# All column-tiled leftovers of an FFN in one place, four live transposed chunks, and edits in the first ten microseconds

## Chip, core and metric

The kernel runs on one core of one Trainium2 chip. The metric is device microseconds of one execution. "PE" is TensorE's matmul row in a profile, "PEld" its weight loads, "DVE" VectorE, "ACT" ScalarE, "POOL" GpSimd, "SPq" the queue that issues transfers. PSUM is the memory that TensorE writes its products to. "Before" and "after" are the two profiled kernels.

## What is computed

A layer norm of x (2048 x 512), then the sum of x, a diagonal state-space branch and a SwiGLU feed-forward branch on the normed x:

```python
xn = _layernorm(x, axis=-1)
# branch A: h[t] = Lam_bar * h[t-1] + (xn @ B_bar^T)[t]; complex, 512 states
y  = 2.0 * einsum("blp,dp->bld", hseq, Cmat).real + xn * Dskip
# branch B: F = 1376
f  = (silu(xn @ w_gate) * (xn @ w_up)) @ w_down
return x + y + f
```

1376 is ten tiles of 128 and a leftover of 96. The kernel computes in bf16 with float32 accumulation, in four chunks of 512 positions, each of four tiles of 128. Below, xn is the normed x and xnT its transpose, "the scan" the recurrence h, and "the down product" the one with w_down.

## The kernel before

A small list scheduler orders every engine's instructions; TensorE and the transfer queue keep program order. Three parts matter.

Leftovers. The 96 leftover gate columns are filled up to 128 with 32 of the leftover up columns. The other 64 up columns are **column-tiled**: two chunks are multiplied at once, one into PSUM partitions 0 to 63, one into 64 to 127. It is done once for chunks 0 and 1, once for 2 and 3:

```python
def ffn_left(c):
    bk = next_pair()
    for k in range(2):                     # L839: full width, 4 matmuls per chunk
        ... e.matmul(pbank[:, bk + k, :], lhsT=wg[:, kt, FL*128:FT*128], rhs=xnT[:, (c + k) % 2, :, kt, :], ...)
    bu = next_pair()
    def mmu(e):                            # L849: 64 columns, two chunks side by side
        for kt in range(KT):
            for k in range(2):
                inst = e.matmul(pbank[64*k:64*k + NU0, bu, :], lhsT=wu[:, kt, FL*128:FL*128 + NU0],
                                rhs=xnT[:, (c + k) % 2, :, kt, :], ...)
    ...                                    # ACT evacuates, DVE multiplies into hT[:, :, FL, :]
```

Program order (cut):

```python
ffn_gate_quarters([0, 1, 2, 3])            # the head: chunk 0's first gate products, tile by tile
...
u1 = ssm_b_chunk(1)
ffn_left(0)
xt_chunk_dma(2)                            # transposed chunk 2 takes the buffer of chunk 0
...
dc_chunk(0)
...
ln_chunk(3); xt_chunk_dma(3)
...
dc_chunk(1)
...
ffn_left(2)
```

Head. Chunk 0's four tiles are normed and transposed on TensorE, between 128-column gate matmuls. Tile 0 is normed half by VectorE, half by ScalarE. Each pair of transposes needs the PSUM slot that ScalarE empties of the pair before. Until there is data, TensorE runs filler matmuls to bring its clock up.

```python
xt_tile_fine(0, 0, wbank)
pe_warm(1, 256, tiles[-2][1])
xt_tile_fine(0, 1)
pe_warm(1, 256, tiles[-2][1])
# (tile quarter, k, position among the gate tiles) -> (x tile, half) to be transposed there
place = {(0, 2, 4): (1, 0), (1, 0, 2): (1, 1), (1, 2, 2): (2, 0), (2, 0, 2): (2, 1), (2, 2, 1): (3, 0), (3, 0, 1): (3, 1)}
```

## Time and profile before

| | before |
|---|---|
| time, median of 3 runs | 179.07 us (179.02 to 179.21) |
| span of the profiled run | 177.7 us |
| PE / DVE / ACT busy | 98% / 92% / 49% |
| first, last matmul | 0.83, 175.11 us |
| clock of TensorE full from | 6.23 us |

The page says that PE bounds the kernel. Whether PE's time is dense, the prediction reads from the trace.

### The profile page before, as it was taken

To read this page: it belongs to the slowest core of one execution; us is meant where nothing else is said; L and a number is where in the kernel's file an instruction comes from. 1 tells how busy PE (TensorE), PEld (TensorE's weight loads), DVE (VectorE), ACT (ScalarE), POOL (GpSimd) and SP (SyncE) were. 2 spreads that over 40 slices of the span, in tenths; PEclk is the share of its full clock that TensorE was granted. 3 is DMA by queue.
4 is the path that set the end of the run, shared out by engine and by line. 5 is a ranking of instruction groups with operands and counts; after the bars stand their busy time and mean duration, and the time that the engine had idled before them with its cause. 6 is when DMAs were issued, how large, how long until landed. Compare 5 with 4: busy or idle time off the path is not lost.

```text
span 177.7 us, 2429 instructions
## 1 busy us (share of the span) xinstructions
PE 174.5 (98%) x935; PEld 84.3 (47%) x935; DVE 162.7 (92%) x284; ACT 87.6 (49%) x116; POOL 10.2 (6%) x22
## 2 busy tenths in 40 slices
PE   8999999999999999999999999999999999999994
PEld 2894444444444444444444444444444444444743
DVE  2865999999999999999999999999999999999933
ACT  4679979899999591052565560000965520000000
POOL 3040500040000000400000000000000000000000
DMA  5892795664956000002600000002000000001122
GB/s 161 268 371 80 132 133 112 163 131 102 348 127 48 0 0 0 0 30 92 120 0 0 0 0 4 0 24 93 1 0 4 0 0 0 0 0 35 36 81 89
DMA packets 22966, 12.37 MB, mean 70 GB/s; under 512 B 15180, under 2 KB 22956, under 8 KB 22956
## 3 DMA queue, kind: packets, MB, share of 16 engines
q1 hardware_dynamic: 22652, 11.77, 26.4%
q10 hardware_dynamic: 304, 0.46, 0.8%
q8 instruction: 7, 0.11, 0.3%
q14 instruction: 3, 0.02, 0.0%
HBM read 6.46 MB, written 2.10 MB: 48 GB/s over the span
## 4 chain that ended last, share of the span: by engine, by line
PE 98%; DVE 0%; issue 0%
PE pb L759 36%; PE pb L959 21%; PE pb L972 16%; PE pb L876 16%; PE pb L803 4%; PE pb L477 3%; PE pb L839 2%; PE pb L849 1%; PE pb L582 1%; DVE x_sb L977 0%
## 5 line engine op out<-in xcount | busy, mean ns | idle before, releaser
L916 DVE TENSOR_TENSOR_SCAN rot<-sm,car,rot 128x512 bf16<-128x512 f32 x32 | 38.8, 1265 | 0.1
L959 PE MATMUL pb<-wd,hT 128*128 128x512 bf16 (+3 forms) x198 | 38.8, 355 | 0.0
L759 PE MATMUL pb<-xnT,wu 128*128 128x512 bf16 x160 | 37.3, 379 | 0.0
L759 PE MATMUL pb<-xnT,wg 128*128 128x512 bf16 x132 | 31.3, 379 | 0.0
L972 PE MATMUL pb<-W,hss 128*128 128x512 bf16 (+2 forms) x144 | 28.3, 355 | 0.0
L876 PE MATMUL pb<-xnT,BT 128*128 128x512 bf16 x128 | 28.1, 379 | 0.0
L959 PEld LDWEIGHTS pb<-wd,hT 128*128 128x128 bf16 (+1 forms) x198 | 18.5, 98 | 19.9
L771 ACT ACTIVATE sg<-pb 128x1024 bf16<-128x1024 f32 x20 | 20.1, 1023 | 9.6 <-PE pb L759 8.7
L759 PEld LDWEIGHTS pb<-xnT,wu 128*128 128x128 bf16 x160 | 15.7, 98 | 18.9 <-issue 0.2
L829 ACT ACTIVATE uf<-pb 128x1024 bf16<-128x1024 f32 x20 | 20.5, 1024 | 7.8 <-PE pb L759 6.8
L972 PEld LDWEIGHTS pb<-W,hss 128*128 128x128 bf16 x144 | 13.5, 98 | 14.3
L759 PEld LDWEIGHTS pb<-xnT,wg 128*128 128x128 bf16 x132 | 12.7, 98 | 15.7 <-issue 0.8
L876 PEld LDWEIGHTS pb<-xnT,BT 128*128 128x128 bf16 x128 | 12.5, 98 | 15.1
L883 ACT ACTIVATE u_sb<-pb 128x1024 bf16<-128x1024 f32 x16 | 16.2, 1016 | 4.4 <-PE pb L876 4.4
L977 DVE TENSOR_TENSOR x_sb<-pb,x_sb 128x512 bf16<-128x512 f32 (+2 forms) x18 | 11.1, 624 | 4.3 <-PE pb L972 4.1
L831 DVE TENSOR_TENSOR hT<-sg,uf 128x1024 bf16<-128x1024 bf16 x20 | 13.5, 681 | 0.8 <-ACT uf L829 0.6
L506 ACT ACTIVATE xn_sb<-x_sb,nmr,rstd 128x512 bf16<-128x512 bf16 x8 | 5.9, 802 | 10.2 <-DVE nmr L503 10.2
L858 ACT ACTIVATE sg<-pb 96x1024 bf16<-96x1024 f32 x2 | 2.0, 1020 | 17.1 <-PE pb L839 17.1
L907 DVE TENSOR_TENSOR rot<-rot,cosT 128x2048 bf16<-128x2048 bf16 x8 | 9.7, 1214 | 0.1
L907 DVE TENSOR_TENSOR rot<-rot,sin 128x2048 bf16<-128x2048 bf16 x8 | 9.7, 1218 | 0.0
L907 DVE TENSOR_TENSOR rot<-u_sb,cosT 128x2048 bf16<-128x2048 bf16 x8 | 9.7, 1216 | 0.0
L907 DVE TENSOR_TENSOR rot<-u_sb,sin 128x2048 bf16<-128x2048 bf16 x8 | 9.7, 1216 | 0.0
(81 smaller groups left out, 143.3 us busy)
## 6 DMA issues: line engine op xcount, KB each, us to landing
out_dram<-x_sb SPq DMA_DIRECT2D x15, 128.0 KB, 1.7
x_sb<-in_A_x_dram SPq DMA_DIRECT2D x3, 512.0 KB, 7.1
wd<-in_B_w_down_dram SPq DMA_DIRECT2D x1, 1280.0 KB, 6.4
wu<-in_B_w_up_dram SPq DMA_DIRECT2D x1, 768.0 KB, 5.3
wu<-in_B_w_up_dram SPq DMA_DIRECT2D x1, 608.0 KB, 7.4
x_sb<-in_A_x_dram SPq DMA_DIRECT2D x4, 128.0 KB, 3.3
wg<-in_B_w_gate_dram SPq DMA_DIRECT2D x1, 480.0 KB, 6.3
wg<-in_B_w_gate_dram ACTq DMA_DIRECT2D x1, 448.0 KB, 3.9
```

The source lines that it names most:

```text
L759: inst = e.matmul(pbank[0:fs, bk, :].rearrange("p (j t) -> p j t", j=4), lhsT=w[:, kt, i * 128:i * 128 + fs], rhs=xnT[:, c % 2, :, kt, :], ...
L771: g.add("act", lambda e: e.activation(out=sg[rows, sl, 0:n, :].rearrange("p a t -> p (a t)"), in_=pair_f32(rows, bk, 512 * n), func=AF.Sil ...
L803: inst = e.matmul(pbank[:, bk, q * 128:(q + 1) * 128], lhsT=wg[:, kt, i * 128:(i + 1) * 128], rhs=xnT[:, 0, q, kt, :], start=(kt == 0), st ...
L829: g.add("act", lambda e: e.activation(out=uf[rows, ul, 0:n, :].rearrange("p a t -> p (a t)"), in_=pair_f32(rows, bk, 512 * n), func=AF.Ide ...
L831: g.add("dve", lambda e: e.tensor_tensor(out=hT[rows, hb, i0:i0 + n, :], in0=sg[rows, sl, 0:n, :], in1=uf[rows, ul, 0:n, :], op=ALU.mult), ...
L876: inst = e.matmul(pbank[:, bk, :].rearrange("p (j t) -> p j t", j=4), lhsT=BT[:, ri, kt, pt * 128:(pt + 1) * 128], rhs=xnT[:, c % 2, :, kt ...
L883: g.add("act", lambda e: e.activation(out=u_sb[:, us].rearrange("p r t -> p (r t)"), in_=pair_f32(slice(0, 128), b0), func=AF.Identity), r ...
L907: tt = lambda out, a, b, op, r, w, nm: g.add("dve", lambda e: e.tensor_tensor(out=out, in0=a, in1=b, op=op), reads=r, writes=w, name="%s_% ...
L916: g.add("dve", lambda e, A0=A0, A1=A1, k=k, ri=ri, pt=pt: e.tensor_tensor_scan(out=A1[:, k, ri, :], data0=rr[:, pt:pt + 1].to_broadcast([1 ...
L959: inst = e.matmul(pbank[:, bk, 0:nc_], lhsT=hT[0:fs, hb, i, lt * 128:(lt + 1) * 128], rhs=wd[0:fs, i, c0:c0 + nc_], start=(i == 0), stop=F ...
L972: inst = e.matmul(pbank[:, bk, 0:nc_], lhsT=hss[:, hb, pt, ri, lt * 128:(lt + 1) * 128], rhs=W12[:, ri, pt, c0:c0 + nc_], start=False, sto ...
L977: g.add("dve", lambda e, bk=bk, a=a, c0=c0, nc_=nc_: e.tensor_tensor(out=x_sb[:, a, c0:c0 + nc_], in0=pbank[:, bk, 0:nc_], in1=x_sb[:, a, ...
```

## The change

Its intent: do the column-tiled matmuls of all four chunks in one run. That needs chunks 0 to 3 transposed and alive at the same time (so four xnT: that of chunk 2 lies in table scratch, that of chunk 3 in a buffer that first holds the iota), chunk 3's x, norm and transpose much sooner, and the down weights later. Two edits of the head come along, and with that of tile 0 a third, small one: tile 1's statistics in one instruction.

```diff
-        xnT = sb("xnT", [128, 2, 4, KT, 128], B16)
+        xnT01 = sb("xnT", [128, 2, 4, KT, 128], B16)
+        xnT3 = sb("xnT3", [128, 4, KT, 128], B16)
+        xnT2 = scrC[:, 2048:3072].bitcast(B16)...          # aliases table scratch; xnT3 also serves as iota
+        xnT = [xnT01[:, 0], xnT01[:, 1], xnT2, xnT3]
...
@@ loads_stage_b2
             dma("ld_x8", ...)
+            dma("ld_x12", ...)
+            dma("ld_dsk", ...)
             dma("ld_cre", ...); dma("ld_cim", ...)
-            dma("ld_wd0", ...); dma("ld_wd1", ...); dma("ld_x12", ...); dma("ld_dsk", ...)
...
@@ head
-            cs = slice(h * 256, (h + 1) * 256)
+            cs = slice(0, 384) if a == 0 else slice(h * 256, (h + 1) * 256)
...                                                          # ScalarE: columns 384:512 instead of 256:512;
...                                                          # tile 1's statistics in one instruction, not two
-            place = {..., (1, 2, 2): (2, 0), ...}
+            place = {..., (1, 2, 1): (2, 0), ...}
...
@@ ffn_left
-        def ffn_left(c):
+        def ffn_left():                                      # all gate leftovers, then all column-tiled ones
+            for c in (0, 2): ... 8 full-width matmuls
+            for c in (0, 2): ... 8 column-tiled matmuls
...                                                          # result in hL; the down product of it now comes
...                                                          # just before the scan outputs (mmB), not last of mmA
@@ program order
         u1 = ssm_b_chunk(1)
-        ffn_left(0)
         xt_chunk_dma(2)
+        dma("ld_wd0", ...); dma("ld_wd1", ...)
...
         resid_chunk(0)
+        ln_chunk(3)
+        xt_chunk_dma(3)
+        ffn_left()
         dc_chunk(0)
...
         resid_chunk(1)
-        ln_chunk(3)
-        xt_chunk_dma(3)
...
-        ffn_left(2)
```

The number of matmuls stays 935.

## The prediction

> **What bounds the kernel now.** I read first the page of the profile: shares of busy time and the chain that ended last.
>
> ```profile
> span 177.7 us, 2429 instructions
> PE 174.5 (98%) x935; PEld 84.3 (47%) x935; DVE 162.7 (92%) x284; ACT 87.6 (49%) x116; POOL 10.2 (6%) x22
> PE 98%; DVE 0%; issue 0%
> ```
>
> The chain is PE from 0.83 us to 175.34 us. "Busy" alone proves little, since the ends of matmuls are modelled, so I listed the start-to-start distance of every matmul in the trace. Warm, a 128x512 matmul follows its predecessor after 0.216 us and a 128x128 one after 0.056 us. Past the head, and apart from the narrower matmuls of the end, that holds everywhere except around the two blocks of column-tiled leftovers. So PE never waits for DVE, ACT or a DMA after 13 us: only fewer PE slots, cheaper PE slots or an earlier head can shorten this kernel. I looked for these in the timeline.
>
> The two leftover blocks (L839 full-width gate part, L849 column-tiled up part, then the next L759), from the timeline:
>
> ```profile
> 38.13 1.89 PE L839 MATMUL pb<-xnT,wg 128*128 128x512 bf16 x8
> 39.95 1.05 PE L849 MATMUL pb<-xnT,wu 128*64 128x512 bf16 x8
> 40.93 1.90 PE L759 MATMUL pb<-xnT,wg 128*128 128x512 bf16 x8
> ...
> 122.13 1.89 PE L839 MATMUL pb<-xnT,wg 128*128 128x512 bf16 x8
> ...
> 123.95 1.05 PE L849 MATMUL pb<-xnT,wu 128*64 128x512 bf16 x8
> ...
> 124.94 0.61 PE L759 MATMUL pb<-xnT,wg 128*128 128x512 bf16 x2
> ```
>
> Subtract the starts. The eight full-width ones take 39.95-38.13 = 1.82 us, where 8 x 0.216 = 1.73 would do: 0.09 too much. The eight half-width ones run as four pairs (the two of a pair start 3 ns apart) and take 0.98 us, where 4 x 0.216 = 0.86 would do: 0.12 too much. Each block so costs about 0.21 us beyond its work, and the second repeats the first.
>
> The head, tiles 0 and 2 of the first chunk, from the timeline:
>
> ```profile
> 4.42 0.35 DVE L517 TENSOR_SCALAR xn_sb<-x_sb,mv,rstd 128x256 bf16<-128x256 bf16 x1
> ...
> 4.74 0.60 ACT L548 ACTIVATE xn_sb<-x_sb,nm,rstd 128x256 bf16<-128x256 bf16 x1
> ...
> 4.84 0.42 PE L582 MATMUL pb<-ident,xn_sb 128*128 128x128 bf16 x2
> ...
> 5.39 0.13 PEld L582 LDWEIGHTS pb<-ident,xn_sb 128*128 128x128 bf16 x2 [0.30 <-ACT xn_sb L548]
> ...
> 8.95 0.83 PE L803 MATMUL pb<-xnT,wg 128*128 128x128 bf16 x12
> 9.15 0.45 ACT L592 ACTIVATE xnT<-pb 128x128 bf16<-128x128 bf16 x2 [0.62 <-PE pb L582]
> ...
> 9.74 0.27 PE L582 MATMUL pb<-ident,xn_sb 128*128 128x128 bf16 x2
> ```
>
> Tile 0's second half waits for ScalarE: it ends at 4.74+0.60 = 5.34 us and PE starts at 5.40. Tile 2's second transposes start at 9.74, but the twelve matmuls before them take only 12 x 0.056 = 0.67 from 8.95, to 9.62. The 0.12 us between is a wait for the PSUM slot that ScalarE empties at 9.15+0.45 = 9.60.
>
> **What the Trainium skill says.** "TensorEngine Tiling (Array Packing)", Key Properties: a change of tiling mode drains TensorE. This trace agrees: 0.310 us instead of 0.216 at entry into the column-tiled run, 0.237 for its first pair, 0.313 at exit, and no extra between later pairs. "TensorE: Matmul & The Clock Gate", the section on 56 ns: warm spacing 55.6 and 215.7 ns, cold 106.7 ns; the trace agrees, with 107 ns for 128 columns until 6.23 us and 56 after. The same page, "What's actually happening": the cold phase is a budget of time (about 3.4 us), not a number of matmuls. The trace shows 5.4 us of cold from the first matmul, longer; I keep only that it is time. "VectorE: DVE Perf Modes", the errata section: instructions on SBUF pay a fixed cost on top of their width. The trace agrees: VectorE's normalisation repeats after 0.262 us at 256 columns and 0.324 at 512, ScalarE takes 0.599 and 0.805.
>
> **The change, part by part.**
>
> 1. Leftovers in one place. Removed from PE: nothing in number (16+16 leftover matmuls stay; the down-projection's leftover matmul moves from before the scan outputs to their group). But 16 column-tiled matmuls now run in a row, so one entry and one exit go: (0.310-0.216)+(0.237-0.216)+(0.313-0.216) = 0.21 us, all on the path, since PE is the path.
>
> 2. Tile 0, 384 to VectorE and 128 to ScalarE. VectorE: +128 columns at (0.324-0.262)/256 a column = +0.03 us, so the first transposes go from 4.84 to 4.87. ScalarE: -128 columns at (0.805-0.599)/256 = -0.10, so its part ends at 5.24. PE can then do the first two transposes and a warm filler, 4.87+0.21+0.21 = 5.30, and goes on at once instead of at 5.40. Two cold transposes and one filler later (2 x 0.107+0.213) the first real matmul starts at 5.73 instead of 5.80. These 0.07 us are cold: if the clock rises at a fixed time, the work pulled ahead is worth half, 0.04 us. Tile 1's statistics in one instruction (0.73 to the next, against 0.78 for two) pay back VectorE's 0.03.
>
> 3. Tile 2's transposes one gate tile (two matmuls, 0.11 us) sooner: ScalarE empties the slot that much sooner and the 0.12 us wait goes. Its input is ready (VectorE ends at 8.53, the new place is about 8.7 us). Tile 3's next transposes wait for a ScalarE square root that is queued behind the same evacuation, so they move too. Worth 0.12, about.
>
> 4. Chunk 3's normalisation, xnT3, x12 and dsk earlier, wd later, aliases instead of own buffers: no PE work. Worth 0 if nothing comes late.
>
> Sum: 0.21+0.04+0.12 = 0.37 us. From 179.07: **178.7 us**.
>
> **Does anything come late?** I laid out the new PE order with the spacings above, shifted by the head's 0.16: FFN of chunk 1 at 37.97, third B product at 37.97+80 x 0.216 = 55.2, leftovers at 62.15, of which chunk 3's gate matmuls (after 12) at 64.7, down-projection at 67.5, first product with the scan outputs at 67.5+40 x 0.216+0.22 = 76.4.
>
> Transfers: x8 landed alone at 32.7; with x12 and dsk behind it I estimate 34.9, from two thirds of a MB at the 0.33 MB/us of the wd group. The two transposes of C then land at about 44 instead of 41.9. The transpose of chunk 2, 5.6 us as before, lands near 50 (needed at 55.2); wd, 6.4 us, near 56; chunk 3's transpose near 62, needed at 64.7. Slack about 3 us.
>
> ```profile
> 50.53 1.69 SPq L397 DMA_TRANSPOSE xnT<-xn_sb x1
> ...
> 67.98 1.22 DVE L609 TENSOR_TENSOR xn_sb<-xn_sb,dsk 128x2048 bf16<-128x2048 bf16 x1
> 69.23 1.22 DVE L611 TENSOR_TENSOR x_sb<-xn_sb,x_sb 128x2048 bf16<-128x2048 bf16 x1
> 70.37 2.46 DVE L482 BATCH_NORM_STATS2 st<-x_sb 128x6 f32<-128x512 bf16 x4
> 72.75 0.36 DVE L486 BATCH_NORM_AGGREGATE mv<-st 128x2 f32<-128x6 f32 x4
> ```
>
> VectorE: chunk 3's statistics and, as its xn tiles reuse chunk 0's slots, chunk 0's residual (these four lines, 5.3 us together) must now run before about 57 us instead of 68 to 73. All this work was done by 74.2, before the products with the scan outputs at 74.6; with the second leftover product (0.69) it ends near 74.9, and is needed at 76.4. Slack 1.5 us.
>
> **The rivals.** (a) The new order of VectorE or the chained transfers makes PE wait once before the leftovers or before the scan outputs. For it: VectorE has no idle time from 38 to 74 us, and the slacks are 1.5 and 3 us. Against it: the total of VectorE's work is unchanged and the deadline moves back by 1.6 us. It would add 0.2 to 2 us: 178.9 to 180.7. (b) Only the leftovers count, the head's gain being eaten by the clock's rise or by tile 3's chain (VectorE ends at 10.36, PE wants it at 10.4): 0.21 us, 178.85. (c) The head gains fully and the drain of a longer column-tiled run costs no more: 0.4 to 0.5 us, 178.6.
>
> **Range and chances.** Before, three runs span 0.19 us. I give (a) one chance in five, most of it below 0.6 us, and the rest to (b), (c) and the sum. Range 178.4 to 179.3. Over 2% would need 3.6 us: no part has that much to give, and a loss as large needs a stall beyond every one that I can lay out. Faster 1%, slower 1%, within 2% 98%.
>
> **What would show it.** Right: one column-tiled run of 16 taking about 1.94 us in all; no gap before tile 2's second transposes; the first L759 matmul at about 12.93 instead of 13.09; PE's share still 98%; the last matmul near 175.0. Wrong: a PE gap before the gate matmuls of chunk 3, with the transpose of chunk 3 landing after 64 us, or before the first product with the scan outputs, with VectorE busy up to it; or a PE end that moved by less than 0.2 us.

## The result

The changed kernel took 178.75 us (median of 6, 178.60 to 179.04), the kernel before beside it 179.17 us (6 runs, 179.02 to 179.37). A ratio here is the mean time of one kernel's fast runs over that of the other's of the same rounds, so not quite the ratio of the medians: 0.9978, 95% interval 0.9966 to 0.9991. So 0.42 us less in the medians; 0.37 had been forecast, 178.7 in time. The interval excludes 1.

Page and chain of the changed kernel:

```profile
span 177.0 us, 2416 instructions
PE 173.3 (98%) x927; PEld 84.0 (47%) x935; DVE 162.8 (92%) x283; ACT 87.4 (49%) x116; POOL 11.0 (6%) x22
PE 98%; issue 0%; DVE 0%
```

PE bounds it as before. The 927 are not fewer matmuls: all 935 weight loads are there, and eight matmul records are missing, seven of them seen as a distance of 0.43 to 0.44 us where 0.216 belongs, the eighth in the lines that follow.

The leftovers, from the chain in order of time (start, duration, what):

```profile
62.02 3.45 PE pb L845 x16
65.47 1.85 PE pb L855 x16
67.32 0.16 issue
67.48 8.58 PE pb L966 x39
```

Sixteen column-tiled matmuls in a row take 1.85 us, their entry included. The issue gap and the 39 are one missing record: 40 matmuls are in the program, and the distance at the exit, 0.537 us, is two distances, which the complete trace of a_again has as 0.312 and 0.227.

The head, from the timeline:

```profile
4.49 0.38 DVE L518 TENSOR_SCALAR xn_sb<-x_sb,mv,rstd 128x384 bf16<-128x384 bf16 x1
...
4.82 0.49 ACT L549 ACTIVATE xn_sb<-x_sb,nm,rstd 128x128 bf16<-128x128 bf16 x1
...
4.92 0.37 PE L585 MATMUL pb<-ident,xn_sb 128*128 128x128 bf16 x2
...
5.36 0.11 PEld L585 LDWEIGHTS pb<-ident,xn_sb 128*128 128x128 bf16 x2 [0.20 <-ACT xn_sb L549]
...
8.52 0.94 PE L806 MATMUL pb<-xnT,wg 128*128 128x128 bf16 x14
8.72 0.45 ACT L595 ACTIVATE xnT<-pb 128x128 bf16<-128x128 bf16 x2 [0.52 <-PE pb L585]
...
9.30 0.28 PE L585 MATMUL pb<-ident,xn_sb 128*128 128x128 bf16 x2
```

Fourteen matmuls from 8.52 take 14 x 0.056 = 0.78, to 9.30, and tile 2's second transposes start at 9.30: the wait of 0.12 us is gone. Its forecast is confirmed by this line alone. But the two traces differ by more than the change: last matmul 175.11 before and 174.43 after, 0.68 us. The part from the first full-width gate weight load to the last matmul ("body" below) shrank from 162.073 to 161.838 us, 0.235; the head gave 0.44, more than forecast. The clock rose by 5.36 us here and at 6.23 in the trace of before. Two traces cannot say whether the change did that.

Chunk 3 and the scan outputs, from the timeline:

```profile
54.82 1.99 SPq L400 DMA_TRANSPOSE xnT<-xn_sb  x1
...
72.07 0.74 DVE L737 SCALAR_TENSOR_TENSOR W<-hss,sm,scrC 128x512 bf16<-128x512 bf16 x1
72.73 0.68 DVE L872 TENSOR_TENSOR hL<-sg,uf 96x1024 bf16<-96x1024 bf16 x1
...
76.12 1.89 PE L980 MATMUL pb<-W,hss 128*128 128x512 bf16 x8
```

Chunk 3's transpose, issued at 54.82, landed at 59.06; TensorE wants it at 64.45. VectorE is done with everything for the scan outputs at 73.4; TensorE takes them at 76.12. The rival of a late transfer or a late VectorE did not occur.

### The profile page after: what moved, and what is told of

Read it like the earlier page. It is cut to its first block, busy times and chain, and to the rows that moved or that the text cites. A ratio compares the mean times of both kernels' runs of the same rounds, so it can differ in the third digit from the quotient of the medians.

```text
span 177.0 us, 2416 instructions
## 1 busy us (share of the span) xinstructions
PE 173.3 (98%) x927; PEld 84.0 (47%) x935; DVE 162.8 (92%) x283; ACT 87.4 (49%) x116; POOL 11.0 (6%) x22
## 4 chain that ended last, share of the span: by engine, by line
PE 98%; issue 0%; DVE 0%
PE pb L762 36%; PE pb L966 19%; PE pb L883 16%; PE pb L980 16%; PE pb L806 4%; PE pb L478 3%; PE pb L977 2%; PE pb L845 2%; PE pb L855 1%; PE pb L585 1%; DVE x_sb L985 0%
## 5 line engine op out<-in xcount | busy, mean ns | idle before, releaser
L966 PE MATMUL pb<-wd,hT 128*128 128x512 bf16 (+2 forms) x176 | 34.5, 355 | 0.3 <-ACT uf L870 0.2
L762 PE MATMUL pb<-xnT,wu 128*128 128x512 bf16 x120 | 27.9, 379 | 0.0
L966 PEld LDWEIGHTS pb<-wd,hT 128*128 128x128 bf16 x180 | 16.8, 98 | 18.2 <-issue 0.4
L762 PE MATMUL pb<-xnT,wg 128*128 128x512 bf16 x92 | 21.8, 380 | 0.0
L883 PE MATMUL pb<-xnT,BT 128*128 128x512 bf16 x96 | 21.0, 379 | 0.0
L762 PEld LDWEIGHTS pb<-xnT,wu 128*128 128x128 bf16 x120 | 11.7, 98 | 14.2 <-ACT sg L774 0.2
L883 PEld LDWEIGHTS pb<-xnT,BT 128*128 128x128 bf16 x96 | 9.4, 98 | 11.3
L762 PEld LDWEIGHTS pb<-xnT,wg 128*128 128x128 bf16 x92 | 9.0, 98 | 10.6
L483 DVE BATCH_NORM_STATS2 st<-x_sb 128x6 f32<-128x512 bf16 x12 | 7.5, 680 | 2.7 <-DMA x_sb<-in_A_x_dram 2.7
L914 DVE TENSOR_TENSOR rot<-rot 128x2048 bf16<-128x2048 bf16 x8 | 9.6, 1219 | 0.0
```

What stands on the lines that cost most here:

```text
L483: return g.add("dve", lambda e, a=a: e.bn_stats(out=st[:, a % 8, :], in_=x_sb[:, a, :]), reads=[("x", a)], writes=[("st", a % 8), ("st0", ...
L762: inst = e.matmul(pbank[0:fs, bk, :].rearrange("p (j t) -> p j t", j=4), lhsT=w[:, kt, i * 128:i * 128 + fs], rhs=xnT[c][:, :, kt, :], sta ...
L883: inst = e.matmul(pbank[:, bk, :].rearrange("p (j t) -> p j t", j=4), lhsT=BT[:, ri, kt, pt * 128:(pt + 1) * 128], rhs=xnT[c][:, :, kt, :] ...
L914: tt = lambda out, a, b, op, r, w, nm: g.add("dve", lambda e: e.tensor_tensor(out=out, in0=a, in1=b, op=op), reads=r, writes=w, name="%s_% ...
L966: inst = e.matmul(pbank[:, bk, 0:nc_], lhsT=hT[0:fs, hb, i, lt * 128:(lt + 1) * 128], rhs=wd[0:fs, i, c0:c0 + nc_], start=(i == 0), stop=F ...
```

## The experiments

Twelve runs; each four share a chip and the runs of the kernel before. The theory: TensorE is the path, and the gain is the sum of its freed slots (leftovers, tile 2, tile 0). The rivals: the clock's rise moved; the reordered transfers did it; the head's gain is eaten further on.

### The kernel before, and the changed kernel, unchanged (b_same, a_same)

> The kernel before, unchanged, timed against itself. It gives the noise of a ratio, and a second trace of where TensorE's clock rises. In the profiled run of before the start-to-start distance fell from 107 to 56 ns at 6.23 us, in that of the changed kernel at 5.37 us. Theory (sum of TensorE slots: leftovers 0.21, tile 2 0.12, tile 0 0.04 us): ratio 1.000 within 0.001, and the clock's rise falls anywhere between about 5 and 7 us, unrelated to the kernel. Rival (the change made the clock rise sooner, and that is the gain): this trace shows the rise at 6.2 us again.

> The changed kernel again. Theory: ratio 0.9979 (0.37 us), confidence interval about 0.001 to each side; the rise of the clock need not be at 5.4 us again. Rival (the change moves the clock's rise): rise at 5.4 us again while the kernel before keeps 6.2 us, and the ratio nearer 0.996, as the two profiled spans (177.7 and 177.0 us) have it.

b_same: 179.28 us against 179.39 (the median of nine runs of before), ratio 0.9994 (0.9981 to 1.0006). a_same: 178.86 us, ratio 0.9969 (0.9956 to 0.9981), a gain of 0.53 us in the medians. The clock's rise in all fourteen traces is no property of a kernel. It is read from the matmul distances, mostly as the start of the first matmul at the short distance, so it can lie up to 0.25 us earlier where a wait or a long filler came before; the profiler's own record of the clock, which seven of the traces hold, agrees within 0.1 us.

| trace | clock rises at, us | first full-width gate weight load, us | body, us |
|---|---|---|---|
| before | 6.23 | 13.04 | 162.07 |
| b_same | 3.5 | 12.65 | 162.29 |
| b_heads | 5.99 | 12.74 | 162.07 |
| after | 5.36 | 12.59 | 161.84 |
| a_same | 5.97 | 12.78 | 161.84 |
| a_again | 3.75 | 12.60 | 161.84 |
| a_eight | 5.1 | 12.62 | 163.43 |
| a_x12late | 5.66 | 12.77 | 169.40 |
| a_two | 5.73 | 12.64 | 162.17 |
| a_t2late | 5.73 | 12.89 | 161.84 |
| a_t0half | 4.6 | 12.48 | 162.34 |
| i_im | 6.38 | 12.98 | 161.84 |
| i_oldhead | 5.73 | 12.75 | 161.84 |
| i_nf_t1 | 4.3 | 12.52 | 161.84 |

The first matmul starts at 0.83 us in all of them. The rival that the change moved the rise falls: the same kernel shows 6.23 and 3.5 us, the changed one 5.36, 5.97 and 3.75. The 3.5 us lie outside the 5 to 7 that were expected. The table also tells how to use the traces: the body is the same to 0.004 us in each undisturbed trace of one kernel, so it resolves what the times do not, while heads may be compared only at like rises.

One thing in b_same was not expected. Its body is 0.22 us longer than that of before. There TensorE, early because of the early rise, reached the first product with B's imaginary part at 24.79 us, and the transfer that brings the transposed imaginary part of B ("B's imaginary transpose" below) landed only at 24.95: a distance of 0.423 us instead of 0.216. More on that below.

### Eight column-tiled runs instead of one (a_eight)

```diff
-   g0 x4, g1 x4, g2 x4, g3 x4, then (u pair) x8
+   g0 x4, g1 x4, then 8 times: one gate matmul of chunk 2 or 3, one column-tiled pair
```

> The changed kernel with the same 32 leftover matmuls, but the eight column-tiled pairs now each stand alone between full-width gate matmuls: eight column-tiled runs instead of one. Theory (each run pays entry 0.094, first pair 0.021 and exit 0.096 us, and time follows TensorE): 7 x 0.21 = 1.47 us more than the changed kernel, so about 180.2 us, ratio to before 1.006. Rival (the drain that the trace shows is hidden or is a matter of the record, and time does not follow it): within 0.2 us of the changed kernel, ratio 0.998 to 0.999.

180.50 us, ratio 1.0062 (1.0046 to 1.0078); 1.64 us more than a_same. From the timeline of this kernel:

```profile
64.26 0.39 PE L839 MATMUL pb<-scrC,wg 128*128 128x512 bf16 x1
64.58 0.41 PE L844 MATMUL pb<-xnT,wu 128*64 128x512 bf16 x2
64.92 0.39 PE L839 MATMUL pb<-scrC,wg 128*128 128x512 bf16 x1
```

A full-width matmul and a pair should take 2 x 0.216 = 0.43 us together; from 64.26 to 64.92 they take 0.66, so 0.23 for going in and out. The body is 1.59 us longer, 0.227 for each of seven more runs (0.21 expected). Time follows TensorE one for one; the rival falls.

### Two column-tiled runs in the same place (a_two)

```diff
-   g0, g1, g2, g3, u(0,1), u(2,3)
+   g0, g1, u(0,1), g2, g3, u(2,3)
```

> The changed kernel with the column-tiled leftovers of chunks 0 and 1 put before the gate leftovers of chunks 2 and 3: two column-tiled runs in the same place, nothing else. Theory: the trace shows two entries of 0.31 us and two exits, and the stretch from the first chunk's first up matmul to the last matmul is 0.2 us longer than the changed kernel's 161.84 us, as the kernel before has it (162.07); time 178.95 to 179.1, ratio 0.998. Rival (the gain of the body comes from the new order of the transfers or of the other engines, not from the mode switch): the stretch stays at 161.84 us.

179.14 us (178.85 to 179.92), ratio 0.9998 (0.9979 to 1.0017): too wide to say whether it is faster or slower than before. The trace decides. From its timeline:

```profile
63.83 1.05 PE L844 MATMUL pb<-xnT,wu 128*64 128x512 bf16 x8
64.81 1.04 PE L839 MATMUL pb<-scrC,wg 128*128 128x512 bf16 x4
...
66.64 0.40 PE L844 MATMUL pb<-scrC,wu 128*64 128x512 bf16 x1
```

Two entries of 0.309 us and two exits of 0.312. The body is 162.166 us. One wait for B's imaginary transpose is in it, 0.101 us in two distances (0.307 and 0.226 where 0.216 belongs); without it the body is 162.065, against 161.840 with one run and 162.073 in the kernel before. So 0.225 of the 0.235 us that the body gained is the second run of column tiling, and the reordered transfers and engines gave at most 0.01.

### The last x tiles loaded late again (a_x12late)

```diff
             dma("ld_x8", ...)
-            dma("ld_x12", ...); dma("ld_dsk", ...)
...
         dma("ld_wd0", ...); dma("ld_wd1", ...)
+        dma("ld_x12", ...); dma("ld_dsk", ...)
```

> The changed kernel with the loads of x12 and of dsk moved back behind the two loads of the down weights, as they were before. Theory (that part is worth nothing by itself, but keeps chunk 3 from being late for the merged leftovers): the last x tiles land near 54 us instead of 34, statistics, root, normalisation and transpose need some 12 us more, so chunk 3's transpose lands near 67 us against the 64.5 us at which TensorE wants it: a wait of 2 to 4 us before chunk 3's leftover gate matmuls, ratio 1.010 to 1.020. Rival (the order of the loads is neutral, there is slack enough): no wait, ratio as the changed kernel's.

186.40 us, ratio 1.0388 (1.0361 to 1.0414), two to four times the expected loss. The waits of PE, and then its timeline:

```profile
PE pb L843 <- DMA xnT<-xn_sb: 5.9, 1, 5.9
```

```profile
70.68 1.89 PE L843 MATMUL pb<-xnT,wg 128*128 128x512 bf16 x4 [5.85 <-DMA xnT<-xn_sb]
72.50 1.70 PE L853 MATMUL pb<-xnT,wu 128*64 128x512 bf16 x8
```

The direction was right, the size not. x12 landed at 55.8 us and dsk at 56.1, near the 54 expected, but the transpose landed at 70.6, not 67: the chain in order of time has the statistics to 59.4, the residual of chunk 0 (which needs dsk and must leave the slots first) to 62.1, a product of the scan to 63.2, ScalarE's normalisation to 66.3. And after 5.9 us without work the clock was low again: the four matmuls from 70.68 follow each other at 0.40 to 0.43 us, and 0.216 comes back at 74.0. The body is 7.56 us longer than a_same's: 6.0 of wait, the rest cold. So the load order is worth nothing as such, and yet without it the merged leftovers cost 7.5 us.

### Tile 2's transposes at their old place (a_t2late)

```diff
-(1, 2, 1): (2, 0)
+(1, 2, 2): (2, 0)
```

> The changed kernel with tile 2's first transposes back at their old place, two matmuls later. Theory: the 0.12 us gap before tile 2's second transposes comes back in the trace, and the time rises by about 0.1 us, at the edge of what the rounds resolve. Rival (tile 3's normalisation or the landing of B's second transpose then holds TensorE, so that the gap was worth nothing): the gap comes back, but the start of the first B product with the imaginary part does not move, since that transpose lands at 24.2 to 24.9 us whatever TensorE does.

From its timeline:

```profile
8.81 0.83 PE L806 MATMUL pb<-xnT,wg 128*128 128x128 bf16 x12
9.60 0.27 PE L585 MATMUL pb<-ident,xn_sb 128*128 128x128 bf16 x2
```

8.81 + 12 x 0.056 = 9.48, so the 0.12 us are back, as forecast. The rival's wait for B's imaginary transpose did not occur in this trace: it landed at 24.91 us, and TensorE came at 25.03. The time, 179.39 us (ratio 1.0007, 0.9992 to 1.0022), is 0.03 us above the kernel before; with the other gains in place it should have stayed some 0.25 us below. The profiled run is the fastest of the five (179.04), and the others near 179.4 left no trace; a wait of 0.14 us for the gate weights in the trace is part of the head's spread. Why these runs were so slow stays open, but the record has a clue. The four list a mean granted clock of 0.999, the profiled run 1.000; of the fourteen traces, a_x12late with its long wait apart, only that of i_im has 0.999, and its clock rose last, at 6.38 us (its own clock record: full from 6.40 to 177.06 us). A rise 0.65 us later than in the profiled run would cost about half of that, 0.3 us (an estimate from the 107 and 56 ns), most of the difference of 0.34 to 0.40. No trace of these four was kept to show it.

### Tile 0 split in halves again (a_t0half)

```diff
-            cs = slice(0, 384) if a == 0 else ...      # ScalarE: 384:512
+            cs = slice(h * 256, (h + 1) * 256)          # ScalarE: 256:512
```

> The changed kernel with tile 0 split 256 and 256 again. Theory: ScalarE's part takes 0.60 instead of 0.49 us, tile 0's second transposes start 0.06 to 0.10 us later counted from VectorE's first instruction, the first gate matmul 0.03 to 0.07 us later; the time does not resolve it (0.04 us). Rival: the first transposes of tile 0, which wait for VectorE, come 0.03 us sooner and the first gate matmul waits for ScalarE's copy of them rather than for the second half, so that it does not move or comes sooner.

Counted from VectorE's first statistics, tile 0's second transposes start at 2.453 us here, as in before (2.452) and b_same (2.453), and at 2.345 in after and a_again: 0.108 us, as forecast. In the early-clock traces the first gate matmul comes 0.11 us later (2.685 against 2.576 in a_again). But the head as a whole, to the first full-width gate weight load, takes 9.595 against 9.582 us. In a_again TensorE, early with tile 0, then waits 0.05 us before tile 1's transposes, and 0.02 before tile 2's; here it does not. So tile 0's edit was worth 0.01 us where the clock is up early. The time, 179.09 us (178.76 to 179.60; ratio 0.9991), resolves nothing. From this trace:

```profile
23.98 0.81 PE L883 MATMUL pb<-xnT,BT 128*128 128x512 bf16 x3
25.12 0.60 PE L883 MATMUL pb<-xnT,BT 128*128 128x512 bf16 x2 [0.33 <-DMA BT<-in_A_B_im_dram]
```

Here is the second floor: B's imaginary transpose landed at 25.07 us, and TensorE, which would have come at 24.62 (24.74 in the trace of after), lost 0.49 us (0.709 instead of 0.216 between the two starts).

### The kernel before with the edits of the head alone (b_heads)

```diff
+ (1, 2, 1): (2, 0); tile 0 split 384 and 128
```

> The kernel before with only the two changes of the head: tile 0 split 384 and 128 with the transposes' waits that this needs, and tile 2's transposes two matmuls sooner (tile 1's statistics stay in two halves). Theory: the gap of 0.12 us is gone, 0.16 us saved, ratio 0.999; the body stays at 162.07 us or is longer by what the landing of B's imaginary transpose takes back. Rival (head gains are swallowed by that landing): ratio 1.000, with a wait of 0.1 us or more before the first matmul with B's imaginary part.

179.18 us against 179.36, ratio 0.9997 (0.9983 to 1.0011). The medians agree with the theory (0.18), the interval with both. In the trace the gap is gone and the body is 162.070, with no wait at B's imaginary transpose. Inconclusive in time. Tile 1's statistics in one instruction were tested by no run of their own; this run goes without, and its trace shows 0.01 us of wait before tile 2's second transposes where a_same, at a like rise, shows none.

### B's imaginary part needed later (a_again, i_im, i_oldhead)

```diff
 chunk 0:
-   re(0), im(0), re(1), im(1), re(2), im(2), re(3), im(3)
+   re(0), re(1), im(0), im(1), re(2), re(3), im(2), im(3)
```

What was expected of the three, in this order:

> The changed kernel a third time, on the chip of the next three runs, as their base. Theory now: its time is the later of two things plus a fixed rest: TensorE's own arrival at the first product with B's imaginary part (24.5 to 24.9 us in the traces so far) and the landing of that transpose (24.3 to 25.1 us in eight traces). So ratio 0.997 to 0.999 with a spread of some 0.4 us from run to run.

> The changed kernel with one more edit: chunk 0's B products run real parts of two tiles first, then the imaginary parts, so that TensorE needs B's imaginary transpose 0.86 us (four matmuls) later. Theory (that landing is a floor under the gain of the head): no trace shows a wait there any more, the body from the first full-width gate matmul to the last one is 161.84 us as in the changed kernel's undisturbed traces, and the mean time falls by 0.05 to 0.2 us below the changed kernel's, with less spread. Rival (the waits of 0.1 and 0.5 us seen in two traces were rare, or another landing right behind takes their place, that of chunk 1's transpose near 29.5 us, wanted near 30.7): same time as the changed kernel within 0.05 us.

> The same with both edits of the head undone (tile 0 split 256 and 256, tile 2's transposes two matmuls later). Theory: with the floor away, the head's gain shows whole: 0.16 us slower than the run with only the reordered B products, the 0.12 us gap back in the trace. Rival (the head edits are worth nothing even then): within 0.05 us of it.

a_again 178.84 us (ratio 0.9976, 0.9955 to 0.9997), i_im 178.79 (0.9970, 0.9952 to 0.9989), i_oldhead 178.89 (0.9978, 0.9959 to 0.9996). Neither trace with the new order waits there. But a_again did not wait either (landing at 24.47), and at the landings of i_im and i_oldhead (24.72 and 24.78) the old order would not have waited: TensorE could have come at 25.12 and 24.90. Only i_nf_t1 below was spared a wait, of 0.06 us (24.72 against 24.66). And 0.05 us less is within noise, nor did the spread shrink (0.50 against 0.53 us): the floor is real in single traces, what it costs on average is not settled. i_oldhead shows its 0.12 us gap and is 0.10 us slower than i_im, 0.16 expected; again the sign and size fit, the intervals overlap. A better comparison of heads is at the same rise of 5.73 us: i_oldhead (old head) takes 9.81 us from VectorE's first statistics to the first full-width gate weight load, a_two (new head) 9.67. So 0.14 us. With an early clock, b_same 9.73 and a_again 9.58: 0.15.

### A try at a faster one (i_nf_t1)

```diff
 # on top of i_im
             xt_tile_fine(0, 1)
-            pe_warm(1, 256, tiles[-2][1])
-(1, 0, 2): (1, 1)
+(1, 0, 3): (1, 1)
```

> The changed kernel with the reordered B products, with tile 1's second transposes one matmul later, and without the second warm filler before the first gate matmul: a try at a faster kernel. Theory: the 0.03 us gap before tile 1's second transposes goes, and where the clock is still low the filler's 0.21 us are replaced by a wait of some 0.05 us for ScalarE's copy; together 0.05 to 0.15 us less than with the reordered B products alone. Rival: without the filler the clock rises later, or ScalarE's copy holds the first gate matmul anyway; same or slower.

178.83 us (ratio 0.9970, 0.9952 to 0.9988), the same as i_im. The gap before tile 1's second transposes did not go: 0.06 us where 0.03 were, one matmul later. Without the filler the first gate matmul came 2.65 us after VectorE's first statistics, against 2.58 in a_again, at a similarly early clock, so nothing was won there either. Both terms of the theory failed. No version here clearly beats the changed kernel.

## Why the prediction was right, point by point

**What bounds.** PE, dense except around column tiling and in the head. Right: bodies agree to 0.004 us, and 1.59 us more of PE in a_eight gave 1.64 us more time.

**Step 1, leftovers, forecast 0.21 us.** Right, a little small: 0.235 in the body, 0.225 when a_two put the second run back, 0.227 a run in a_eight. The forecast added three distances and left out two small ones that the runs of column tiling in before and a_two show: the 3 to 4 ns between the two matmuls of a pair, and 0.010 us in the distance after the exit (0.226 instead of 0.216). With them it is 0.227. The last 0.008 us of the body's 0.235 I cannot place.

**Step 2, tile 0, forecast 0.04 us.** The mechanism was right and to the point (ScalarE's part 0.49 us, VectorE's 0.03 longer, second transposes 0.108 earlier for 0.10 forecast). Its worth was assigned to the wrong limit: "work pulled ahead is worth half" was meant for a late clock, and no pair of traces at like late rises tests it. With an early clock the 0.11 us reach the first gate matmul whole, then 0.07 of it is seen again as waits before later transposes, and the end of the head gains 0.01. At the rise of 5.73 us, i_oldhead against a_two leave 0.02 us for it beside tile 2's 0.12. So this term was too large by 0.02 to 0.03 us.

**Step 3, tile 2, forecast 0.12 us.** Right in every trace: 0.119 to 0.120 us in the four with the old place, at most 0.02 us in the ten others.

**Steps 2 and 3 together,** 0.16 forecast, 0.14 to 0.15 at like rises.

**Step 4, no worth if nothing is late.** Right, by a_two. The layout of times was near but pessimistic: chunk 3's transpose landed at 59.1 (forecast 62) for 64.5 (64.7), VectorE was done at 73.4 (74.9) for 76.1 (76.4). The transfers gained most: the last x tiles and dsk landed by 35.2 us (34.9 estimated), but the down weights were in at 54.7 instead of 56, so the chained transpose was issued sooner, at 54.8, and it took 4.2 us where that of chunk 2 had taken 5.6 before. Chunk 2's, at 48.4 instead of 50, gave the down weights their start. a_x12late shows that this was no idle worry.

**Rival (a)**, a stall: did not occur in any trace of the changed kernel. **Rival (b)**, the head's gain eaten: true in single traces, but by something not on the list. The floor is the landing of B's imaginary transpose, 24.3 to 25.1 us in fourteen traces, while TensorE, with the order of products that both kernels have, wants it at 24.6 to 25.2. Three traces waited there, a_two 0.09, b_same 0.21 and a_t0half 0.49 us, but none of the three of the changed kernel itself. The prediction laid out deadlines only after the merged leftovers and missed this one before them. **Rival (c)**, more: the profiled pair's 0.68 us looked like it; the head of b_same, the kernel before with an early clock, starts its full-width gates at 12.65 us instead of 13.04 without any change, so a surplus of this size is within what the clock's rise does.

**Sum.** 0.235 from the body and about 0.14 from the head make 0.375 us; forecast 0.37. That the sums agree so closely is partly luck: step 1 was too small by about as much as step 2 was too large. Three timings gave 0.42, 0.53 and 0.31 us in the medians, ratios 0.9978, 0.9969 and 0.9976.

**Signs named beforehand.** The column-tiled run at 1.94 us: 1.85 with its entry, and 0.10 at its exit, right. Gap gone: right. The first full-width gate matmul near 12.93 and the last matmul near 175.0: they came at 12.65 and 174.43, off by the clock's rise, which moves a head by up to 0.4 us and which no sign of this kind should have been hung on.

## What to carry to other kernels

When TensorE is dense, sum start-to-start distances against their nominal value; what is over is what a reordering can win; here such a sum forecast 0.37 us where 0.31 to 0.53 were timed. Gather instructions that change TensorE's tiling mode into one run, but count what must be alive and early for it: the enabling loads were worth nothing and their absence cost 7.5 us. Compare traces of a short effect by a stretch that excludes the clock's rise, and look for the next transfer behind every wait that you remove.

## What the Trainium skill lacked or had wrong

- "TensorE: Matmul & The Clock Gate", What's actually happening: a cold budget of about 3.4 us, said to vary by 0.5 us either way. Here it is 2.7 to 5.6 us from the first matmul, for heads that start alike in fourteen traces, and it moves the first full-width gate matmul by up to 0.4 us. After 5.9 us without work it was cold again for 3.3 us, which agrees with the page.
- The same page, Back-to-back issue gap: about 131 ns a matmul sustained at N=512 with weight loads. Here every 128x512 matmul at full clock with its own weight load follows its full-width predecessor after 0.216 us, never less than 0.214; that is the page's own 215.7 ns of the section on 56 ns.
- "TensorEngine Tiling (Array Packing)", Key Properties: says that a mode switch drains, without a size. Here 0.09 us at the entry, 0.02 for the first pair, 0.10 at the exit and 0.01 after it; 0.23 us for a run in all.
- "DMA: Bandwidth & Descriptors", DMA Transpose: no time for a transfer of the size here (elsewhere the page has effective rates and sequencer cycles, no duration). A transpose of 512 x 512 bf16 from DRAM (the two of B) landed 3.9 to 4.3 us after its issue, and the second of them between 24.3 and 25.1 us in kernels with the same load order, enough to hide or show the head's gain.
